# Fixed slots after the first two chunks in a routed mixture of experts behind a gated recurrence

## Chip, cores and metric

The kernel runs on one core of a Trainium2 chip. The metric is the device time of one execution in microseconds (us), lower is better; the median of several runs is compared.

## What is computed

A gated linear recurrence runs over 4 sequences of 5056 tokens with 256 features. Its 20224 output rows go through a mixture of 8 experts, where each token visits only the expert with the largest logit:

```python
log_a = c * sig_r * np.log(np.clip(a_base, 1e-06, 1.0 - 1e-06))[None, None, :]
a_t = np.exp(log_a)
x_gated = np.sqrt(np.maximum(1.0 - a_t * a_t, 1e-06)) * sig_i * x
for t in range(S):
    h = a_t[:, t] * h + x_gated[:, t]
    y[:, t] = h
...
logits = x @ w_gate                      # x: the 20224 rows of y
e_idx = np.argmax(logits, axis=1)
for e in range(E):
    mask = e_idx == e
    h = np.maximum(x[mask] @ w1[e], 0.0)      # 256 -> 1024
    ye = h @ w2[e]                            # 1024 -> 256
    out[mask] = gate_w[mask, None] * eom[mask, e, None] * ye
```

## The kernel before

**Chunks.** The 158 tiles of 128 tokens are cut into 20 chunks of 8 tiles (the last has 6). `chunk` loads the three inputs of half a chunk (`rt`, `it`, `xt`, 0.5 MB each), makes the gates on ScalarE (ACT) and VectorE (DVE), runs the recurrence as a scan on DVE, and then, tile by tile, transposes on TensorE (PE) against an identity that also carries the router's columns (`prow`). DVE and ACT split each row into a high and a low half of fp16 (`rows_all`), choose the expert, rank each token within its expert (`pk`, `posi`), and GpSimd (POOL) scatters the rows by an indirect DMA into `xs`, a table in device memory with one region of rows for each expert.

**Slots.** A slot is a piece of up to 256 or 128 rows of one expert. The counts are known only on the chip, so `plan` (DVE) works out for a group of slots which expert and which row each one takes; tokens that do not fill a slot wait for a later chunk. `slot` then fetches the rows with a transposing DMA (`xt16`), copies the expert's first weights (`ws`, two copies of 0.5 MB, from `w1r` in on-chip memory at an address read from the plan), multiplies 48 times for the first layer (`ph`), evacuates each fourth of it by a `relu` on ACT and a `low` on DVE (`h`), multiplies 24 times for each 128 rows for the second layer (`po`), scales on ACT (`ot`) and scatters the result on POOL. A slot of 256 rows is called wide here, one of 128 narrow. Before the change there are 63 wide and 39 narrow slots: 17 narrow ones after chunks 1 and 2, four wide ones after each of chunks 4 to 18, and 3 wide and 22 narrow ones at the end. The last 3 narrow slots stand under an `If` and run only if the first of them has rows.

**Weights.** Each of the 16 weight matrices (8 experts, two layers; 1 MB each) is a `unit`: it is loaded, measured (a Gram product on PE, `pg`, then a square on ACT and two small steps on DVE, `wsc`), and split into a high half (ACT, or DVE where `MODES` has a D) and a low half (DVE) that stay on the chip in `w1r` and `w2r`. Before, the first layers of all experts come first, then the second layers, and the first slot's weight copy waits for all first layers, its second layer for all units.

**Order.** Every step is a `work` item with a rank. `in_order` lays the items out on the engines by a planner whose costs are tables at the head of the file (`UNIT_RANK`, `CHUNK_RANK`, `SLOT_RANK` and so on). PE, ACT and DVE then run exactly in that order; SP's and POOL's queues follow it too. An engine therefore stands still when the next row of its list is not ready.

## Time and profile before

| | |
|---|---|
| median of 3 runs | 1089.17 us (1087.86 to 1091.37) |
| the profiled execution: its own time | 1083.89 us |
| its span, first to last instruction | 1082.2 us |
| PE / DVE / ACT / POOL busy | 990.1 / 732.1 / 633.8 / 345.7 us |
| mean granted clock of PE | 0.965 |

The profile is of one execution. Its own time lies 1.7 us above its span, and 0.5% below the median of the runs, so a sum made on the span has to be scaled to the median. Busy time is a union over an engine's instructions; where short instructions overlap in the pipeline, the sum of their durations is larger than the busy time.

### The profile page before, as it was taken

To read this page: it belongs to the slowest core of one execution; us is meant where nothing else is said; L and a number is where in the kernel's file an instruction comes from. 1 tells how busy PE (TensorE), PEld (TensorE's weight loads), DVE (VectorE), ACT (ScalarE), POOL (GpSimd) and SP (SyncE) were. 2 spreads that over 40 slices of the span, in tenths; PEclk is the share of its full clock that TensorE was granted. 3 is DMA by queue.
4 is the path that set the end of the run, shared out by engine and by line. 5 is a ranking of instruction groups with operands and counts; after the bars stand their busy time and mean duration, and the time that the engine had idled before them with its cause. 6 is when DMAs were issued, how large, how long until landed. Compare 5 with 4: busy or idle time off the path is not lost.

```text
span 1082.2 us, 29773 instructions
## 1 busy us (share of the span) xinstructions
PE 990.1 (91%) x9738; PEld 897.1 (83%) x9738; DVE 732.1 (68%) x2012; ACT 633.8 (59%) x1092; POOL 345.7 (32%) x346
## 2 busy tenths in 40 slices
PE   2445689999999999999999999999999999999997
PEld 2434578888998989989889899989999988899997
DVE  7999987869757777676777758677687544234332
ACT  9885866766756556566665657757565333223332
POOL 1033133233332423333243333334434444122111
PEclk9867699999999999999999999999999999999999
DMA  9992499999768697796968779787675555447993
GB/s 346 392 367 85 116 265 278 321 308 288 247 207 257 192 249 208 238 222 222 257 220 224 225 224 253 215 243 243 215 239 169 177 182 186 155 155 223 233 243 131
DMA packets 196862, 249.41 MB, mean 230 GB/s; under 512 B 120013, under 2 KB 128976, under 8 KB 196720
## 3 DMA queue, kind: packets, MB, share of 16 engines
q1 hardware_dynamic: 180928, 204.17, 64.4%
q0 software_dynamic: 15792, 43.31, 12.0%
q8 instruction: 94, 1.54, 0.6%
q14 instruction: 48, 0.39, 0.1%
...
## 4 chain that ended last, share of the span: by engine, by line
PE 41%; issue 20%; DMA 10%; POOL 8%; DVE 6%; SPq 3%; ACT 3%; POOLq 0%; ACTq 0%
PE po L933 19%; PE ph L889 19%; POOL xs L339 5%; DMA xs<-rows_all,posi 4%; DMA rt<-in_r_gate_dram 4%; POOL out_dram L948 3%; PE prow L598 3%; DVE h L907 2%; DMA ws<-w1r 1%; SPq L837 1%; DVE it L564 1%; DMA out_dram<-ot,mt 1%; ACT h L904 1%; ACT rt L511 1%; SPq L838 1%
## 5 line engine op out<-in xcount | busy, mean ns | idle before, releaser
L889 PE MATMUL ph<-xt,ws 128*128 128x256 f16 (+1 forms) x4752 | 524.8, 255 | 19.1 <-DVE h L907 12.2
L933 PE MATMUL po<-w2r,h 128*128 x3888 | 520.4, 273 | 2.4 <-ACT ot L945 0.9
L889 PEld LDWEIGHTS <-ws 128*128 128x128 f16 x4752 | 410.4, 99 | 61.8 <-issue 9.5
L933 PEld LDWEIGHTS <-h 128*128 128x128 f16 x3888 | 374.3, 98 | 44.8 <-issue 2.9
L907 DVE SCALAR_TENSOR_TENSOR h<-ph,h 128x512 f16<-128x512 f32 (+1 forms) x396 | 226.7, 589 | 210.5 <-ACT h L904 208.1
L948 POOL DMA_INDIRECT out_dram<-ot,mt x162 | 175.0, 1080 | 447.5 <-ACT ot L945 386.4
L904 ACT ACTIVATE h<-ph 128x512 f16<-128x512 f32 (+1 forms) x396 | 201.0, 518 | 155.9 <-PE po L933 109.4
L339 POOL DMA_INDIRECT xs<-rows_all,posi x158 | 158.5, 1003 | 270.9 <-ACT h L904 128.0
L598 PE MATMUL prow<-iw,it 128*128 128x144 f32 x632 | 112.2, 306 | 37.0 <-DVE it L564 20.2
L623 ACT ACTIVATE rows_all<-prow,sc 128x256 f16<-128x256 f32 x150 | 68.5, 473 | 116.2 <-DMA xs<-rows_all,posi 93.7
L945 ACT ACTIVATE ot<-po,osc 128x256 f32<-128x256 f32 x162 | 69.7, 471 | 106.5 <-PE po L933 94.4
L598 PEld LDWEIGHTS prow<-iw,it 128*128 128x128 f32 x632 | 92.9, 204 | 40.3 <-issue 32.8
L564 DVE TENSOR_TENSOR_SCAN it<-rt,last,it 128x512 f32<-128x512 f32 (+4 forms) x78 | 95.8, 1241 | 0.5
L627 DVE SCALAR_TENSOR_TENSOR rows_all<-prow,sc,rows_all 128x256 f16<-128x256 f32 x158 | 75.3, 477 | 0.0
L533 DVE SCALAR_TENSOR_TENSOR it<-it,xt 128x1024 f32<-128x1024 f32 (+1 forms) x40 | 48.3, 1207 | 24.0 <-ACT it L530 24.0
L612 DVE TENSOR_REDUCE am<-prow 128x1 f32<-128x256 f32 x158 | 59.5, 416 | 6.5 <-PE prow L598 6.5
L521 ACT ACTIVATE rt<-rt,lam 128x512 f32<-128x512 f32 (+1 forms) x80 | 60.8, 803 | 0.5
L626 DVE COPY lz<-prow 128x16 f32<-128x16 f32 x158 | 26.6, 169 | 50.3 <-ACT rows_all L623 50.1
L517 DVE SCALAR_TENSOR_TENSOR xt<-it,xt 128x1024 f32<-128x1024 f32 (+1 forms) x40 | 48.3, 1207 | 10.8 <-ACT it L514 10.6
L511 ACT ACTIVATE rt<-rt 128x1024 f32<-128x1024 f32 (+1 forms) x40 | 41.8, 1045 | 22.5 <-DMA rt<-in_r_gate_dram 21.5
L514 ACT ACTIVATE it<-it 128x1024 f32<-128x1024 f32 (+1 forms) x40 | 41.8, 1045 | 8.9 <-DMA it<-in_i_gate_dram 8.8
L530 ACT ACTIVATE it<-it,quarter 128x1024 f32<-128x1024 f32 (+1 forms) x40 | 45.2, 1138 | 0.3
...
## 6 DMA issues: line engine op xcount, KB each, us to landing
...
out_dram<-ot,mt POOLq DMA_INDIRECT x162, 3.6
xs<-rows_all,posi POOLq DMA_INDIRECT x158, 3.6
```

The costliest lines, as they stand in the source:

```text
L339: op = nc.gpsimd.indirect_dma_start(out=xs[:, :], out_offset=bass.IndirectOffsetOnAxis(ap=pos, axis=0), in_=rows.bitcast(F32), in_offset=None,
L521: nc.scalar.activation(r[:, h], r[:, h], AF.Exp, scale=lam[:, h:h + 1], bias=lam[:, h:h + 1])
L564: nc.vector.tensor_tensor_scan(H[:, h, lo:hi], A[:, h, lo:hi], H[:, h, lo:hi], first, op0=ALU.mult, op1=ALU.add)
L598: nc.tensor.matmul(pf[:, h * P:(h + 1) * P + 2 * E], lhsT=H[:, h, (j % 4) * P:(j % 4 + 1) * P], rhs=iw[:, h, :], start=h == 0, stop=h == N ...
L623: nc.scalar.activation(r4(j)[:, 0], pr(j), AF.Copy, scale=sc)
L627: nc.vector.scalar_tensor_tensor(r4(j)[:, 1], pr(j), st("sc", 1, I32)[:, j, :].bitcast(F32), r4(j)[:, 0], op0=ALU.mult, op1=ALU.subtract)
L889: nc.tensor.matmul(ph[:, i, 0:w], lhsT=ws[:, f // 2 % 2, a, c, i * P:(i + 1) * P], rhs=xt[:, b * ND + c, 0:w], start=k == 0, stop=k == 3 * ...
L904: newest["relu"] = nc.scalar.activation(part(0, f0), tiles["ph", s, f0][:, :, 0:w], AF.Relu).ins
L907: nc.vector.scalar_tensor_tensor(part(1, f0), tiles["ph", s, f0][:, :, 0:w], 0.0, part(0, f0), op0=ALU.max, op1=ALU.subtract)
L933: nc.tensor.matmul(po[0:pw, j], lhsT=hh[:, a, f % 4, j * P:j * P + pw], rhs=w2r[:, bass.ds(eo + (b * NF + f) * D, D)], start=f + j + a + b ...
L945: nc.scalar.activation(ot[0:pw], tiles["po", s][0:pw, j], AF.Copy, scale=tiles["osc", s][0:pw, j, :])
L948: op = nc.gpsimd.indirect_dma_start(out=out[:, :], out_offset=bass.IndirectOffsetOnAxis(ap=tiles["mt", s][0:pw, j, 1:2].bitcast(I32), axis=0),
```

## The change

After each of the first two chunks there are now 8 narrow slots of fixed place, one for each expert: slot k takes rows 0 to 127 (after chunk 1: rows 128 to 255) of expert k's region. They need no plan, no address registers and no `ws` copy, since place and expert are constants; they read `w1r` and `w2r` directly. So that a region that has too few tokens can be read, two `fill` DMAs write zero rows over the first 256 rows of each region, and the scatters of chunk 0 wait for them; `carry` is raised so that the next tokens go behind the fixed rows. The weights are split expert by expert, three experts ahead of the slots, and each fixed slot waits only for its own expert. Later slots come from a table, `CUTS`: 5 narrow after chunk 2, 7 after chunk 3, then 6, 5 and 4 slots after chunks 4, 5 and 6 to 10 (wide and narrow mixed), four wide ones after chunks 11 to 18, and 38 narrow ones at the end, of which 23 run always, 3 under an `If` and 12 under a second `If` inside it. Wide and narrow slots of a chunk are planned as two groups, and every plan now checks whether a slot is used. Together: 50 wide and 79 narrow slots in place of 63 and 39. The extra bytes are 2 x 1.08 MB of zero rows. Chunk 1 no longer borrows the buffers of `ws` and `hh` for its loads. All tables of ranks are new.

```diff
+STATIC = 2
+
+CUTS = {
+    2: ((128, 5),), 3: ((128, 7),), 4: ((256, 1), (128, 5)), 5: ((256, 2), (128, 3)), 6: ((256, 3), (128, 1)),
+    7: ((256, 3), (128, 1)), 8: ((256, 3), (128, 1)), 9: ((256, 3), (128, 1)), 10: ((256, 3), (128, 1)),
+}
+CUT = ((256, 4),)
+
+ENDS = (23, 3)
+AHEAD = 3
...
-SLOT_RANK = (-35.066, -22.048, -35.396, -20.11)
+SLOT_RANK = (-168.923, -171.768, -182.749, -176.243)
...
-        w = WIDTHS[c] if c < len(WIDTHS) and c < NC - 1 else SLOT
-        pending -= add_slots(c, max(0, -(-(pending - E * (w - 1)) // w)), w)
+        if c < STATIC:
+            add_slots(c, E, P)
+            pending -= min(pending, P)
+        elif c < NC - 1:
+            for w, k in CUTS.get(c, CUT):
+                add_slots(c, k, w)
+                pending = max(min(pending, E * (w - 1)), pending - k * w)
     n_full = len(width)
     add_slots(NC - 1, (pending + E * (P - 1)) // P, P)
     n_slots = len(width)
+    static = {s: (c, k) for c in range(STATIC) for k, s in enumerate(slots_in[c])}
...
+    def fill(r):
+
+        op = nc.sync.dma_start(
+            xs.rearrange("(e r) d -> r e d", e=E)[r * P:(r + 1) * P],
+            zrow.bitcast(F32).rearrange("p (o d) -> p o d", o=1).to_broadcast([P, E, ROW // 2]),
+        )
+        tc.declare_no_dep(op.ins, group="xs", reason="rows of xs are written before those of tokens")
+        tc.add_to_no_dep_group("xs", op.ins)
+        queue("SP", op)
+        scatters.append((-1, op.ins))
...
+        for k in [k for cc, k in scatters if cc < 0] if c == 0 else []:
+            tc.add_manual_dep(
+                ins, k.name, mybir.DependencyInfo(mybir.DependencyClass.Sync, mybir.DependencyReason.DATA),
+                reason="zero rows are written before those of tokens",
+            )
...
-    units = [(e, i) for i in range(2) for e in range(E)]
+    units = [(e, i) for e in range(E) for i in range(2)]
...
-            nc.vector.tensor_tensor(left, left, pk[:, nt * E:(nt + 1) * E], op=ALU.add)
+            if c >= STATIC:
+                nc.vector.tensor_tensor(left, left, pk[:, nt * E:(nt + 1) * E], op=ALU.add)
+                return
+
+            nc.vector.tensor_scalar(tab[:, 3, :], tab[:, 3, :], float(P), None, op0=ALU.add)
+            nc.vector.tensor_tensor(carry, carry, tab[:, 3, :], op=ALU.max)
+            if c == STATIC - 1:
+                nc.vector.tensor_tensor(left, carry, tab[:, 3, :], op=ALU.subtract)
...
-            if tail:
-                a = tile_of("pla", [GROUP, 1])[:, 0:n]
-                nc.vector.tensor_reduce(a, o, axis=AX.X, op=ALU.add)
-                nc.vector.tensor_tensor(v[:, :, 0:1], v[:, :, 0:1], step[w][:, 0:n, 0:1], op=ALU.add)
-                nc.vector.scalar_tensor_tensor(v[:, :, 0:1], v[:, :, 0:1], -float(dummy), a, op0=ALU.add, op1=ALU.mult)
-                nc.vector.tensor_scalar(v[:, :, 0:1], v[:, :, 0:1], float(dummy), None, op0=ALU.add)
-                nc.vector.tensor_copy(vi, v[:, :, 0:2])
-            else:
-                nc.vector.tensor_tensor(vi, v[:, :, 0:2], step[w][:, 0:n], op=ALU.add)
+
+            a = tile_of("pla", [GROUP, 1])[:, 0:n]
+            nc.vector.tensor_reduce(a, o, axis=AX.X, op=ALU.add)
+            nc.vector.tensor_tensor(v[:, :, 0:1], v[:, :, 0:1], step[w][:, 0:n, 0:1], op=ALU.add)
+            nc.vector.scalar_tensor_tensor(v[:, :, 0:1], v[:, :, 0:1], -float(dummy), a, op0=ALU.add, op1=ALU.mult)
+            nc.vector.tensor_scalar(v[:, :, 0:1], v[:, :, 0:1], float(dummy), None, op0=ALU.add)
+            nc.vector.tensor_copy(vi, v[:, :, 0:2])
...
+        w_ = work("DVE", 3.3, emit, [chain["plan"], old] + undone, -4.5 + s0 / 1000, uses=[use])
...
+        for w in sorted({width[s] for s in slots_in[c]}, reverse=True):
+            same = [s for s in slots_in[c] if width[s] == w]
+            if same[0] >= n_full:
+                cuts = [same[:ENDS[0]], same[ENDS[0]:sum(ENDS)], same[sum(ENDS):]]
+            else:
+                cuts = [same]
+            for part in cuts:
+                for k in range(0, len(part), GROUP):
+                    plan(part[k:k + GROUP])
...
-        ready, vuse = planned[s]
-        if s in rescaled:
-            rescaled["last"] = rescaled[s]()
-        scaled = rescaled["last"]
+        fixed = static.get(s)
+        ready, vuse = planned[s] if fixed is None else (counted[c], [])
+        expert = None if fixed is None else fixed[1]
+        scaled = undone[expert] if fixed else None
...
+                row = expert * REGION + fixed[0] * P
+                rows = xs[row:row + w]
...
-        rows = [v for cc in range(c + 1) for v in routed[cc]] if s == 0 or chunk_of[s - 1] != c else list(routed[c])
+        rows = list(routed[c])
...
+        every = [v for u in range(2 * E) for v in split[u]] if s == len(static) else []
...
+                    if fixed is None:
+                        ws = tiles["ws", s, f // 4]
+                    else:
+                        ws = w1r[:, expert * 2 * size + f // 4 * size:][:, 0:size].rearrange(
+                            "p (q h c f) -> p q h c f", q=2, h=2, c=ND
+                        )
...
-                deps = [wf[f0 // 4], fw] + ([pold] if i == 0 else [m])
+                deps = ([wf[f0 // 4]] if fixed is None else split[2 * expert]) + [fw] + ([pold] if i == 0 else [m])
...
-            m = work("PE", 0.327 * q, multiply2, [m, evac[f // 2], ready] + (every if f == 0 else []), rank + LAG + f / 1e4, uses=[pu, hus[f // 4][0], vuse])
+            m = work("PE", 0.327 * q, multiply2, [m, evac[f // 2], ready] + ((every if fixed is None else split[2 * expert + 1]) if f == 0 else []), rank + LAG + f / 1e4, uses=[pu, hus[f // 4][0], vuse])
...
+    fills = [work("SP", DMA_ISSUE, lambda r=r: fill(r), [tb], FILL, dma=3.0) for r in range(STATIC)]
...
-    for c in range(2):
+
+    def unscale(e):
+        nc.vector.reciprocal(undo[:, :, e:e + 1], wsc.bitcast(F32)[:, :, e:e + 1])
+        nc.vector.tensor_tensor(tab[:, 2, e:e + 1], undo[:, 0, e:e + 1], undo[:, 1, e:e + 1], op=ALU.mult)
+
+    def weights_of(e):
+        scaled = [unit(u, STAGED.get(u)) for u in (2 * e, 2 * e + 1)]
+        undone.append(work("DVE", 0.35, lambda: unscale(e), scaled, 3.5))
+
+    counted = {}
+    for c in range(NC):
         chunk(c)
-        plans(c)
-    scaled = [unit(u, STAGED.get(u)) for u in range(2 * E)]
-
-    def unscale():
-        nc.vector.reciprocal(undo, wsc.bitcast(F32))
-        nc.vector.tensor_tensor(tab[:, 2, :], undo[:, 0, :], undo[:, 1, :], op=ALU.mult)
-
-    undone[0] = work("DVE", 0.3, unscale, scaled, 3.5)
-    for c in range(NC):
-        if c > 1:
-            chunk(c)
+        counted[c] = chain["carry"]
+        if c >= STATIC:
             plans(c)
+        if c == 0:
+            for e in range(AHEAD):
+                weights_of(e)
         for s in slots_in[c]:
-            if s >= n_slots - SPARE and not late:
+            if c == 0 and s + AHEAD < E:
+                weights_of(s + AHEAD)
+            if s >= n_full + ENDS[0]:
                 late.append(s)
             slot(s)
...
+    k = n_full + sum(ENDS)
+    with where_used(n_full + ENDS[0]):
```

Where the tables move instructions shows in the order of the engines. The first place is SP's queue ahead of the first fetch of a slot's rows: in these rows `fw` and `w2r` are loads of weights, `ws` the copies of slot 0's weights, `xt_0_988` and `xt_0_579` the rows of slot 0, `mt` their scales, and `pvi` the plan. Before:

```order
L393 DMA fw_1_629<-in_moe_w_dram 128x4x256
L393 DMA fw_0_652<-in_moe_w_dram 128x4x256
L858 TENSOR_LOAD pvi_869
L863 ISA
L863 DMA ws_0_899<-w1r 128x2048
L863 ISA
L863 DMA ws_1_902<-w1r 128x2048
L505 DMA it_4_929<-in_i_gate_dram 128x2x512
L505 DMA xt_0_963<-in_x_dram 128x2x512
L830 TENSOR_LOAD pvi_869
L837 ISA
L837 DMA_TRANSPOSE xt_0_988<-xs 128x4x128
```

Now:

```order
L424 DMA w2r<-in_moe_w_dram 128x8x256
L424 DMA w1r<-in_moe_w_dram 128x2x1024
L424 DMA w2r<-in_moe_w_dram 128x8x256
L424 DMA w1r<-in_moe_w_dram 128x2x1024
L536 DMA xt_0_569<-in_x_dram 128x2x512
L424 DMA w2r<-in_moe_w_dram 128x8x256
L872 DMA_TRANSPOSE xt_0_579<-xs 128x4x128
L873 DMA mt_580<-xs 128x2
L872 DMA_TRANSPOSE xt_1_585<-xs 128x4x128
L873 DMA mt_586<-xs 128x2
L872 DMA_TRANSPOSE xt_2_596<-xs 128x4x128
L873 DMA mt_597<-xs 128x2
```

Slot 0's rows stood behind all loads of weights and behind the copy of its own weights, whose address is read from the plan; now they stand behind 14 of the 16 units, and no plan or copy stands ahead.

The second place is DVE around the first `low` of slot 0 (the row that makes `h_0` from `ph_0`). `lz` and `rows_all` belong to a chunk's rows, `mx` and `df` to its choice of experts. Before:

```order
L466 SCALAR_TENSOR_TENSOR w2r<-fw_0_529,wsc,w2r 128x1024
L466 SCALAR_TENSOR_TENSOR w2r<-fw_1_629,wsc,w2r 128x1024
L626 COPY lz_911<-prow_6_1017 128x16
L627 SCALAR_TENSOR_TENSOR rows_all<-prow_6_1017,sc_825,rows_all 128x256
L626 COPY lz_911<-prow_7_1075 128x16
L627 SCALAR_TENSOR_TENSOR rows_all<-prow_7_1075,sc_825,rows_all 128x256
L647 TENSOR_REDUCE mx_1127<-lz_911 128x8
L648 TENSOR_TENSOR df_1129<-lz_911,mx_1127 128x64
L432 TENSOR_SCALAR wsc<-pg_1082 128x1
L433 TENSOR_SCALAR wsc<-wsc 128x1
L907 SCALAR_TENSOR_TENSOR h_0_1131<-ph_0_1021,h_0_1131 128x2x128
L907 SCALAR_TENSOR_TENSOR h_0_1131<-ph_2_1043,h_0_1131 128x2x128
```

Now:

```order
L598 COPY last_4_631<-it_4_282 128x2
L643 TENSOR_REDUCE am_603<-prow_2_600 128x1
L643 TENSOR_REDUCE am_603<-prow_3_627 128x1
L645 TENSOR_SCALAR sc_604<-am_603 128x2
L548 SCALAR_TENSOR_TENSOR xt_0_569<-it_0_343,xt_0_569 128x1024
L947 SCALAR_TENSOR_TENSOR h_0_658<-ph_0_635,h_0_658 128x2x128
L657 COPY lz_615<-prow_2_600 128x16
L658 SCALAR_TENSOR_TENSOR rows_all<-prow_2_600,sc_604,rows_all 128x256
L657 COPY lz_615<-prow_3_627 128x16
L658 SCALAR_TENSOR_TENSOR rows_all<-prow_3_627,sc_604,rows_all 128x256
L1018 RECIPROCAL undo<-wsc 128x2
L1019 TENSOR_TENSOR tab<-undo 128x1
```

Before, the rows ahead of it are the last units' splits (`fw`) and the choice of experts of chunk 2; now chunk 1 is half done there, and the units of four experts are split (`undo` follows at once).

## Rows read from the trace of the kernel before

**Rows 1.** The page: span, busy time, granted clock in 40 slices of 27 us.

```profile
span 1082.2 us, 29773 instructions
...
PE 990.1 (91%) x9738; PEld 897.1 (83%) x9738; DVE 732.1 (68%) x2012; ACT 633.8 (59%) x1092; POOL 345.7 (32%) x346
...
PEclk9867699999999999999999999999999999999999
```

**Rows 2.** Windows: busy us (instructions) of each engine, granted clock, DMA share, GB/s.

```profile
0.00:80.00 80.00, 30.99 (x213) 28.00 (x213) 69.58 (x164) 68.27 (x91) 13.18 (x26) 0.81 1.02 369
80.00:120.00 40.00, 23.65 (x196) 21.69 (x197) 38.65 (x92) 25.29 (x42) 11.89 (x8) 0.69 0.32 102
120.00:160.00 40.00, 28.47 (x289) 25.84 (x288) 34.00 (x96) 28.96 (x48) 9.13 (x10) 0.79 0.70 201
160.00:200.00 40.00, 36.22 (x442) 33.02 (x441) 33.05 (x95) 28.07 (x52) 14.31 (x14) 0.96 1.05 298
200.00:1000.00 800.00, 794.20 (x7599) 717.28 (x7598) 532.78 (x1501) 456.67 (x794) 281.73 (x274) 1.00 0.76 224
```

**Rows 3.** Timeline of PE: the first slot's first layer (start, us, instruction, idle before).

```profile
117.02 4.00 PE L889 MATMUL ph<-xt,ws 128*128 128x128 f16 x36 [2.11 <-DMA xt<-xs]
...
130.78 1.46 PE L889 MATMUL ph<-xt,ws 128*128 128x128 f16 x12 [6.41 <-DVE h L907]
```

**Rows 4.** Timeline of PE at full clock: a row starts where the last is issued.

```profile
201.19 1.17 PE L889 MATMUL ph<-xt,ws 128*128 128x128 f16 x18
202.19 2.13 PE L933 MATMUL po<-w2r,h 128*128 x18
204.16 0.83 PE L889 MATMUL ph<-xt,ws 128*128 128x128 f16 x12
...
643.11 0.66 PE L598 MATMUL prow<-iw,it 128*128 128x144 f32 x4
643.61 2.13 PE L889 MATMUL ph<-xt,ws 128*128 128x256 f16 x18
645.57 0.82 PE L933 MATMUL po<-w2r,h 128*128 x6
```

**Rows 5.** Groups by form on PE: x count | busy us, mean ns | idle before.

```profile
L933 PE MATMUL po<-w2r,h 128*128 x3888 | 520.4, 273 | 2.4 <-ACT ot L945 0.9 <-ACT h L904 0.8 <-issue 0.7
L889 PE MATMUL ph<-xt,ws 128*128 128x256 f16 x3024 | 393.0, 273 | 3.1 <-DVE h L907 2.5 <-DMA ws<-w1r 0.3 <-DMA xt<-xs 0.2
L889 PE MATMUL ph<-xt,ws 128*128 128x128 f16 x1728 | 131.8, 224 | 16.0 <-DVE h L907 9.7 <-DMA ws<-w1r 3.9 <-DMA xt<-xs 2.1
```

**Rows 6.** Groups by form on DVE.

```profile
L907 DVE SCALAR_TENSOR_TENSOR h<-ph,h 128x512 f16<-128x512 f32 x252 | 169.4, 685 | 125.8 <-ACT h L904 124.6 <-issue 0.8
L564 DVE TENSOR_TENSOR_SCAN it<-rt,last,it 128x512 f32<-128x512 f32 x70 | 88.2, 1275 | 0.4
L627 DVE SCALAR_TENSOR_TENSOR rows_all<-prow,sc,rows_all 128x256 f16<-128x256 f32 x158 | 75.3, 477 | 0.0
L907 DVE SCALAR_TENSOR_TENSOR h<-ph,h 128x256 f16<-128x256 f32 x144 | 57.3, 421 | 84.7 <-ACT h L904 83.5 <-issue 0.7
L466 DVE SCALAR_TENSOR_TENSOR w1r<-w1r,wsc 128x1024 f16<-128x1024 f32 x12 | 14.8, 1280 | 1.1 <-ACT w1r L456 1.1
L466 DVE SCALAR_TENSOR_TENSOR w2r<-w2r,wsc 128x2048 f16<-128x2048 f32 x6 | 14.1, 2346 | 0.0
```

**Rows 7.** Timeline of DVE: first low of slot 0 and of slot 9.

```profile
130.31 0.74 DVE L907 SCALAR_TENSOR_TENSOR h<-ph,h 128x256 f16<-128x256 f32 x2
...
196.87 0.42 DVE L907 SCALAR_TENSOR_TENSOR h<-ph,h 128x256 f16<-128x256 f32 x1 [0.46 <-ACT h L904]
```

**Rows 8.** Timeline of POOL: first and last of chunk 0's eight scatters.

```profile
56.39 0.96 POOL L339 DMA_INDIRECT xs<-rows_all,posi  x1 [46.03 <-DVE am L612]
...
66.29 0.96 POOL L339 DMA_INDIRECT xs<-rows_all,posi  x1 [0.30 <-issue]
```

**Rows 9.** Timeline of PE: the last matmuls.

```profile
1072.63 4.09 PE L933 MATMUL po<-w2r,h 128*128 x36
```

More of the change, by code (lines that the diff above doesn't have):

```diff
@@ L478, in rglru_moe @@
     last_tile = {}
-    planned, rescaled, undone = {}, {}, {}
+    planned, undone = {}, []
     routed = {}
@@ L719, in chunk @@
         ps = work("DVE", 0.85, positions, [pk, chain["carry"]], quick, uses=[pu])
-        ct = work("DVE", 0.17, counts, [ps, chain["carry"]] + ([chain["plan"]] if chain["plan"] else []), quick, uses=[pu])
+        ct = work("DVE", 0.28 if c >= STATIC else 0.65, counts, [ps, chain["carry"]] + ([chain["plan"]] if chain["plan"] else []), quick, uses=[pu])
         chain["carry"] = ct
@@ L735, in chunk @@
             routed["ends"] = [
-                work("Pool", SPREAD[1], lambda e=e: scatter_rows(tiles["ends"][:, e:e + 1], zrow, NC), [w], quick, dma=0.38) for e in range(E)
+                work("Pool", SPREAD[2], lambda e=e: scatter_rows(tiles["ends"][:, e:e + 1], zrow, NC), [w], quick, dma=0.38) for e in range(E)
             ]
@@ L743, in plan @@
         s0, n, w = group[0], len(group), width[group[0]]
-        tail, early = s0 >= n_full, chunk_of[s0] < 2
+        tail = s0 >= n_full
         def tile_of(nm, shape, dt=F32, bufs=1):
@@ L753, in over_k @@
             return t.rearrange("p (o e) -> p o e", o=1).to_broadcast([P, n, t.shape[1]])
-        m = 2 if early else 3
+        m = 3
         def emit():
@@ L803, in plan @@
             planned[s] = (w_, use)
-        rescaled[s0] = lambda: work("DVE", 0.35, scales, [w_, undone[0]], -4.4 + s0 / 1000, uses=[use]) if early else w_
     def plans(c):
-        full = [s for s in slots_in[c] if s < n_full]
-        rest = slots_in[c][len(full):]
-        for group in (full, rest):
-            for k in range(0, len(group), GROUP):
-                plan(group[k:k + GROUP])
+        for w in sorted({width[s] for s in slots_in[c]}, reverse=True):
[7 more added lines that the diff above has]
+                    plan(part[k:k + GROUP])
     def slot(s):
@@ L916, in scales @@
             osc = tiles["osc", s] = small.tile([P, 2, 1], F32, name=f"osc_{s}", tag="osc", bufs=4)
-            nc.vector.tensor_scalar(osc[0:pw, 0:q, :], tiles["mt", s][0:pw, 0:q, 0:1], tiles["scale", s][0:pw], None, op0=ALU.mult)
-        sc = work("DVE", 0.2, scales, [scaled, fw, oold, evac[2]], rank, uses=[vuse, mu, ou])
+            by = tiles["scale", s][0:pw] if fixed is None else tab[:, 2, expert:expert + 1]
+            nc.vector.tensor_scalar(osc[0:pw, 0:q, :], tiles["mt", s][0:pw, 0:q, 0:1], by, None, op0=ALU.mult)
+        sc = work("DVE", 0.2, scales, [scaled, ready, fw, oold, evac[2]], rank, uses=[vuse, mu, ou])
         pu, pold = rings["ps_o"].new()
@@ L988, in rglru_moe @@
             w.emit()
-    newest.clear()
-    (row,) = (nc.values_load(
-        tiles["plan", late[0]][0:1, 0:1], min_val=0, max_val=E * REGION - P,
-        skip_runtime_bounds_check_because="rows are counted on the chip",
-    ),)
     rest = [w for w in works if w.late]
@@ L998, in rglru_moe, with where_used @@
     for w in rest:
-        w.after = [d for d in w.after if (isinstance(d, tuple) or id(d) in kept)]
-        w.after = [([x for x in d[0] if id(x) in kept], [x for x in d[1] if id(x) in kept]) if isinstance(d, tuple) else d for d in w.after]
-    with tc.If(row != dummy):
+        w.after = [d for d in w.after if isinstance(d, tuple) or id(d) in kept]
+        w.after = [tuple([x for x in k if id(x) in kept] for k in d) if isinstance(d, tuple) else d for d in w.after]
+    def where_used(k):
+        newest.clear()
+        row = nc.values_load(
+            tiles["plan", k][0:1, 0:1], min_val=0, max_val=E * REGION - P,
+            skip_runtime_bounds_check_because="rows are counted on the chip",
+        )
+        return tc.If(row != dummy)
+    k = n_full + sum(ENDS)
+    with where_used(n_full + ENDS[0]):
         with tc.manual_schedule(engines=engines):
-            for w in in_order(rest, {}):
+            for w in in_order([w for w in rest if w.late < k], {}):
                 w.emit()
+        if k < n_slots:
+            for w in rest:
+                w.after = [d for d in w.after if isinstance(d, tuple) or d.late >= k]
+                w.after = [tuple([x for x in q if x.late >= k] for q in d) if isinstance(d, tuple) else d for d in w.after]
+            with where_used(k):
+                with tc.manual_schedule(engines=engines):
+                    for w in in_order([w for w in rest if w.late >= k], {}):
+                        w.emit()
 _FEATURE_MAJOR = ("x", "r_gate", "i_gate")
```

112 lines of the change are left out of this document (54 added, 58 removed).

## The prediction

> **What bounds the kernel now.** I read the page first: PE is busy 91% of the span, and the row of its granted clock is low only in the first seven slices, about 190 us [rows 1]. The windows say the same in numbers [rows 2]: from 200 to 1000 us PE is busy 794.2 of 800 us, at full clock; in the first 200 us it is busy only 31.0 + 23.7 + 28.5 + 36.2 = 119.3 us, much of it at a mean granted clock of 0.69 to 0.81, a mixture of the two levels, 1.2 and 2.4 GHz. So two things can change the end: the amount of PE work, and how early PE has enough to do. In the first 200 us DVE is the busy engine (69.6 of 80, 38.7 of 40, 34.0 and 33.1 of 40). The timeline of PE then shows the first slot's multiplications only at 117.0 us, and they wait at 130.8 for a `low` of DVE [rows 3].
>
> **A unit for the sums.** At full clock a matmul costs, start to start [rows 4]: 128 columns (202.19 - 201.19) / 18 = 0.0556 us; `po` (204.16 - 202.19) / 18 = 0.1094 us, and 256 columns the same within 1% (645.57 - 643.61 over 18); the four records of one tile's `prow` 643.61 - 643.11 = 0.50 us. The ranking `pk` of a chunk is about 0.2 us (an estimate, nine short matmuls). A narrow slot is then 48 x 0.0556 + 24 x 0.1094 = 5.3 us, a wide one 96 x 0.1094 = 10.5 us.
>
> **More work for PE.** Before, 3888 matmuls of `po` and 3024 + 1728 of `ph` ran [rows 5]: 162 pieces of 128 rows in 99 slots, 63 wide and 36 narrow; the three under the `If` did not run. For the change I worked out the routing of the reference's data and put it through the table of slots: every planned slot finds a full piece, and 23 pieces are left for the end, exactly those that run always. So 50 wide and 64 narrow slots run, 164 pieces. That is 50 x 10.5 + 64 x 5.3 = 863.7 against 63 x 10.5 + 36 x 5.3 = 852.0: **11.7 us more**, certain, and at full clock, since PE has no idle time later in which to hide it. Two of the fixed slots' pieces are filler. The number of weight copies is nearly unchanged (98 planned slots against 99), so the stage after 200 us has no lighter DMA.
>
> **An earlier start, and who sets it.** DVE executes in the planner's order, so I added up the mean durations (busy over count, from the groups by form; the heaviest are in [rows 6]) of all DVE rows ahead of a given row. Ahead of slot 0's first `low` stand 129.4 us before the change, and the trace starts it at 130.3; ahead of slot 9's stand 195.0 us, and it starts at 196.9 [rows 7]. Up to there this sum reads as a clock: the overlap of short rows makes up for the tenth that DVE is idle. In the changed order the same sum is 68.1 us ahead of slot 0's `low` (21.9 of it splitting weights, 21.7 gates and scans, 12.6 rows of chunks 0 and 1), 130.9 ahead of slot 6's, 196.3 ahead of slot 16's and 292.4 ahead of slot 30's. So at about 196 us slot 16 takes the place that slot 9 had.
>
> From such a point the end follows from the PE work that its order still has ahead. Before, from slot 9's first `po`: 3687 x 0.1094 + 1248 x 0.0556 + 3024 x 0.1094 + 118 tiles x 0.5 + 3.3 = 865.9 us; 196.9 + 865.9 = 1062.8, and the last matmul ended at 1072.63 + 4.09 = 1076.7 [rows 9]. The 13.9 us between are the way from the `low` to the `po`, some 6 us of idle time and small gaps; I carry them over. The span ends 5.5 us after the last matmul; that too stays.
>
> Changed: slot 6, 899.7 us left: 130.9 + 899.7 + 13.9 + 5.5 = 1050.0. Slot 30, left 3192 x 0.1094 + 1614 x 0.0556 + 2352 x 0.1094 + 103 x 0.5 + 2.9 = 750.6: 292.4 + 750.6 + 19.4 = 1062.4. The largest of these counts: slots 20 to 30 of the changed order give 1060 to 1063, later ones less than 1058. So PE waits for DVE until about 290 us, longer than now, because the narrow slots, their plans (17 rows of DVE a group in place of 13, two groups for a mixed chunk) and chunks 2 to 5 all stand in that stretch. **Gain so far 1082.2 - 1062.4 = 19.8 us**, which already holds the 11.7 us.
>
> **What makes the start later than the sum.** DMA: ahead of slot 0's fetch in SP's queue stand 14 units (14.7 MB), 14 half-chunk loads (7.3 MB), the two fills (2.2 MB), and POOL moves 1.1 MB of chunk 0's rows: 25.3 MB, at the 369 GB/s of the first 80 us [rows 2] 68.6 us and some 2 us to begin, an estimate. So the rows of slot 0 land at about 71 to 73 us and the first `low` comes at about 75 to 77, not 68. The scatters do not set it: chunk 0's run from 56.4 to 67.2 us now [rows 8], and the positions that they wait for have 34 us of DVE sum ahead in place of 51, so even with the fills in front they end near 60. I also expect DVE to lie about 9 us behind its sum at the first positions, since with chunk 0 alone ready it waits for ACT's square roots and PE's transposes in turn. DVE can make up some of the 9 us where it is ready throughout (from 80 to 120 us it was busy 97% of the time [rows 2]); bounds are 0 and 9, I take 6, as no stretch of the trace shows it catching up by more than a few us. Span 1062.4 + 6 = 1068.4; own time 1.7 us more, 1070.1; scaled by 1089.17 / 1083.89 to the median, **1075 us**.
>
> Costs that I set at nothing: the three extra DVE rows of `counts` and the per-expert `undo` are in the sum; the second `If` stands inside the first, which is not entered; the extra plan groups at the end (six, not three) lie on DVE when it is far ahead. Without that cover each group would cost about 3 us once.
>
> **A rule that speaks against it.** The first slot ran at half rate: 36 matmuls of 128 columns took 4.00 us, 0.11 each, and the granted clock was 0.69 from 80 to 120 us [rows 2, 3]. The change moves 16 slots into such a stretch, where PE has waits between its bursts. The Trainium skill, "TensorE: Matmul & The Clock Gate", section "What's actually happening", has it that "the default state is throttled, and activity releases the throttle". By that rule, if the new stretch counts as too idle, its work takes up to twice the time; the trace agrees in so far as the clock rose to 0.96 once slots came one upon another. By the rows, PE has 51 us of full-rate work between slot 0 and slot 6 and DVE's sum gives it 63, so a little of this is hidden.
>
> **Rivals.** (a) The gain is larger: DVE catches up wholly after slot 6, and that slot binds: 1050.0 + 9 = 1059 span, 1066 median; with no lateness 1057. For it speaks that DVE's busy time is a tenth below its sum; against it, that the sum was the clock for 197 us. (b) DVE stays the bound. In chunks 6 to 10 its sum is about 40.8 us a chunk, and PE's work 3 x 10.5 + 5.3 + 8 x 0.5 + 0.2 = 41.0; before it was 37 against 46. No wait there is made up. If the order runs 5% behind its sum, slot 54 (sum 509.9, 528 us left) ends at 535.4 + 528 + 19.4 = 1083 span: 1090 median, no gain; at 8% it is 15 us more, slower. The turning point is 5%. For it: `low` waits for ACT's `relu` behind PE, which is already the largest wait of DVE [rows 6]. (c) The clock. If the 51 us run at 0.69, they take 74 and the span is 77 + 74 + 899.7 + 19.4 = 1070, within the forecast; at half clock 102 us, 1098, median **1105, slower**. It decides from a mean clock of 0.59 downward between 75 and 160 us. Against it: at 160 to 200 us the clock was 0.96 with PE 90% busy. (d) The early DMA is slow: at the 298 GB/s of 160 to 200 us [rows 2] the 25.3 MB take 85 us, the first `low` comes at 89, 12 us later, 1080 span, 1087 median: no change.
>
> **Chances.** Forecast 0.55 (median 1066 to 1086), (a) 0.18, (b) 0.14 (half of it slower), (c) 0.08, (d) 0.05. The range from 1058 to 1092 leaves out the tail of (a) below and most of (c) and the far part of (b) above. A measurement of this kernel tells about 0.3% from no change. Faster: the forecast but for its edge, and (a), 0.74; same: (d), part of (b) and that edge, 0.11; slower 0.15.
>
> **What would show it.** Right: first `ph` at 70 to 78 us; slot 16's first `low` near 200; PE's clock at 1.00 from about 140 us; PE busy some 10 us more in total; idle of PE for DVE's `low` spread until about 300 us and hardly any after. Wrong: a first `ph` after 85 us (fetch or fills), a granted clock near 0.5 up to 160 us, waits of PE for `low` that go on through chunk 10 (some 500 us), or the slots under the `If` running.

## The result and the profile after

The changed kernel takes **1078.41 us** (median of 4 runs, 1073.18 to 1081.11) beside 1088.51 us for the kernel before on the same chip: ratio **0.9904**, 95% interval 0.9875 to 0.9932. On a second chip it came to 1069.22 beside 1080.53 us, ratio 0.9886 (0.9870 to 0.9901). The forecast was 1075 us, with a range of 1058 to 1092. The profiled execution is the slowest of the four: own time 1081.11 us, span 1079.4 us. Spans of profiled executions therefore differ by only 2.8 us, where the medians differ by 10.1.

The page after, beside [rows 1]: PE is busy 11.4 us longer, close to the 11.7 us of added work, and the granted clock is low in slices 2 and 3 (27 to 81 us), and again a little in slice 5 (108 to 135 us) and slice 12 (about 300 us).

```profile
span 1079.4 us, 31430 instructions
...
PE 1001.5 (93%) x10506; PEld 910.0 (84%) x10506; DVE 772.4 (72%) x2324; ACT 642.5 (60%) x1153; POOL 361.7 (34%) x348
...
PEclk9659799999989999999999999999999999999999
```

The windows after, same stretches as [rows 2] (busy us of PE, its weight loads, DVE, ACT, POOL; granted clock; DMA share; GB/s):

```profile
0.00:80.00 80.00, 34.81 (x274) 31.27 (x275) 65.41 (x163) 55.75 (x81) 17.52 (x26) 0.74 1.04 349
80.00:120.00 40.00, 34.74 (x456) 32.35 (x454) 36.17 (x84) 32.84 (x62) 18.96 (x12) 0.98 0.59 134
120.00:160.00 40.00, 35.40 (x389) 32.02 (x388) 34.86 (x97) 30.80 (x56) 5.79 (x4) 0.85 0.49 135
160.00:200.00 40.00, 39.38 (x511) 36.79 (x509) 35.95 (x115) 27.17 (x50) 16.21 (x16) 1.00 0.71 177
200.00:1000.00 800.00, 784.79 (x7922) 709.38 (x7921) 568.13 (x1752) 468.85 (x840) 288.45 (x275) 0.99 0.81 237
```

In the first 200 us PE is now busy 144.3 us, against 119.3 before, and from 80 to 200 us at a higher clock (0.98, 0.85 and 1.00 in place of 0.69, 0.79 and 0.96); up to 80 us it is lower, 0.74 in place of 0.81. That is the gain. But from 200 to 1000 us it stands still 15.2 us, against 5.8 before. Cut finer, in the same view, first before, then after:

```profile
200.00:320.00 120.00, 117.17 (x1246) 106.66 (x1245) 90.10 (x268) 78.87 (x141) 39.15 (x39) 1.00 0.92 271
320.00:800.00 480.00, 477.14 (x4387) 429.71 (x4386) 348.79 (x934) 303.21 (x501) 175.47 (x168) 1.00 0.80 231
```

```profile
200.00:320.00 120.00, 110.72 (x1304) 100.44 (x1303) 91.78 (x312) 77.18 (x150) 44.53 (x40) 0.96 0.97 275
320.00:800.00 480.00, 474.28 (x4550) 427.03 (x4548) 388.55 (x1179) 321.16 (x543) 182.23 (x174) 1.00 0.86 247
```

9.3 us idle in the first in place of 2.8 before, 5.7 in the second in place of 2.9. A clock of 0.96 in place of 1.00 over the first 120 us means some 10 us at the lower level, which costs about 5 us more, an estimate. Both are given back, beside the added work. What PE waits for from 200 to 320 us (us in total, times, longest):

```profile
PE prow L629 <- DVE rows_all L658: 3.1, 1, 3.1
PE ph L929 <- DMA ws<-w1r: 2.1, 1, 2.1
PE po L982 <- ACT ot L994: 1.3, 1, 1.3
...
PE ph L929 <- DVE h L947: 0.8, 3, 0.3
```

The marks that the prediction named, in the timeline of DVE after (start, us; first lows of slots 0, 6, 16 and 30):

```profile
74.96 0.42 DVE L947 SCALAR_TENSOR_TENSOR h<-ph,h 128x256 f16<-128x256 f32 x1
...
137.51 0.76 DVE L947 SCALAR_TENSOR_TENSOR h<-ph,h 128x256 f16<-128x256 f32 x2
...
200.84 0.75 DVE L947 SCALAR_TENSOR_TENSOR h<-ph,h 128x256 f16<-128x256 f32 x2
...
304.33 0.75 DVE L947 SCALAR_TENSOR_TENSOR h<-ph,h 128x256 f16<-128x256 f32 x2
```

and in that of PE (start, us, idle before). The first slot comes at 73.00 us; the four `prow` behind a 3.11 us wait run at half rate, 1.12 us from start to start in place of 0.50 [rows 4]; the same again at 300 us. The granted clock is 0.54 from 125.84 to 136 us and 0.51 from 299.95 to 306 us:

```profile
73.00 1.44 PE L929 MATMUL ph<-xt,w1r 128*128 128x128 f16 x12 [1.55 <-DMA xt<-xs]
...
125.84 1.33 PE L629 MATMUL prow<-iw,it 128*128 128x144 f32 x4 [3.11 <-DVE rows_all L658]
126.96 2.15 PE L450 MATMUL pg<-fw 128*128 128x128 bf16 x16
...
299.95 1.33 PE L629 MATMUL prow<-iw,it 128*128 128x144 f32 x4 [3.09 <-DVE rows_all L658]
301.07 0.85 PE L929 MATMUL ph<-xt,ws 128*128 128x128 f16 x6
...
1068.65 3.77 PE L982 MATMUL po<-w2r,h 128*128 x33
```

### The profile page after: what moved, and what is told of

Its sections match the earlier page's. It is cut to its first block, busy times and chain, and to the rows that moved or that the text cites. A ratio compares the mean times of both kernels' runs of the same rounds, so it can differ in the third digit from the quotient of the medians.

```text
span 1079.4 us, 31430 instructions
## 1 busy us (share of the span) xinstructions
PE 1001.5 (93%) x10506; PEld 910.0 (84%) x10506; DVE 772.4 (72%) x2324; ACT 642.5 (60%) x1153; POOL 361.7 (34%) x348
## 4 chain that ended last, share of the span: by engine, by line
PE 59%; issue 10%; DMA 10%; DVE 9%; POOL 5%; ACT 4%; SPq 1%; POOLq 0%; ACTq 0%; DVEq 0%
PE ph L929 27%; PE po L982 27%; PE prow L629 5%; DMA xs<-rows_all,posi 3%; POOL xs L365 3%; DVE it L595 2%; POOL out_dram L997 2%; DVE h L947 2%; DMA rt<-in_r_gate_dram 2%; DMA w2r<-in_moe_w_dram 1%; DMA ws<-w1r 1%; DMA w1r<-in_moe_w_dram 1%; DMA xt<-xs 1%; DVE it L564 1%; ACT h L944 1%
## 5 line engine op out<-in xcount | busy, mean ns | idle before, releaser
L982 PE MATMUL po<-w2r,h 128*128 (+1 forms) x3936 | 533.3, 274 | 3.5 <-ACT ot L994 1.3
L929 PE MATMUL ph<-xt,ws 128*128 128x256 f16 (+1 forms) x4704 | 484.3, 247 | 5.1 <-DMA ws<-w1r 2.1
L929 PEld LDWEIGHTS <-ws 128*128 128x128 f16 x4704 | 384.4, 98 | 42.1 <-issue 4.6
L947 DVE SCALAR_TENSOR_TENSOR h<-ph,h 128x256 f16<-128x256 f32 (+1 forms) x456 | 240.1, 537 | 217.6 <-ACT h L944 187.8
L944 ACT ACTIVATE h<-ph 128x256 f16<-128x256 f32 (+1 forms) x456 | 211.8, 474 | 243.1 <-PE ph L929 150.4
L997 POOL DMA_INDIRECT out_dram<-ot,mt x164 | 180.9, 1103 | 434.6 <-ACT ot L994 313.9
L365 POOL DMA_INDIRECT xs<-rows_all,posi x158 | 168.5, 1066 | 264.3 <-ACT h L944 173.2
L994 ACT ACTIVATE ot<-po,osc 128x256 f32<-128x256 f32 x164 | 71.9, 471 | 54.9 <-PE po L982 49.4
L929 PE MATMUL ph<-xt,w1r 128*128 128x128 f16 x768 | 55.3, 225 | 4.6 <-DVE h L947 2.6
L929 PEld LDWEIGHTS <-w1r 128*128 128x128 f16 x768 | 50.6, 102 | 7.3 <-issue 6.0
```

Of the source, the lines that this page charges most:

```text
L365: op = nc.gpsimd.indirect_dma_start(out=xs[:, :], out_offset=bass.IndirectOffsetOnAxis(ap=pos, axis=0), in_=rows.bitcast(F32), in_offset=None,
L929: nc.tensor.matmul(ph[:, i, 0:w], lhsT=ws[:, f // 2 % 2, a, c, i * P:(i + 1) * P], rhs=xt[:, b * ND + c, 0:w], start=k == 0, stop=k == 3 * ...
L944: newest["relu"] = nc.scalar.activation(part(0, f0), tiles["ph", s, f0][:, :, 0:w], AF.Relu).ins
L947: nc.vector.scalar_tensor_tensor(part(1, f0), tiles["ph", s, f0][:, :, 0:w], 0.0, part(0, f0), op0=ALU.max, op1=ALU.subtract)
L982: nc.tensor.matmul(po[0:pw, j], lhsT=hh[:, a, f % 4, j * P:j * P + pw], rhs=second(b), start=f + j + a + b == 0, stop=f == NF - 1 and a == ...
L994: nc.scalar.activation(ot[0:pw], tiles["po", s][0:pw, j], AF.Copy, scale=tiles["osc", s][0:pw, j, :])
```

## Experiments

A **reading** used below, the prediction's own: the time of a slot's first `low` plus the full-rate PE work that stands behind it in the order. Where it is flat from slot to slot, PE loses nothing; where it rises, PE stood still or ran at half rate. Before it is 1049 us at slot 0, 1066 at slot 9, 1071 at the end. In the changed kernel (profile of the run `again`) it is about 1020 at slots 0 and 5, 1036 at slot 6, 1043 at slot 20, 1050 at slot 30, 1057 at slot 80 and 1061 at the end. So the head start by this reading is some 30 us up to slot 9, and some 20 of it are given back by the end; 8.8 us more idle after 200 us (14.6 against 5.8) and some 5 us for the lower clock, as estimated above, account for 14; the rest is not located. **Theory 1**: the gain is the earlier start, at the pace of DVE's order; DVE goes on to pace later slots and so gives part of it back. Each experiment has its rival. The kernel before ran again beside each group of runs, so times are compared by ratio. The yardstick is 0.9886; the first measurement of the same kernel gave 0.9904, so a difference of 0.2% says little.

**The unchanged kernel as yardstick (`again`).** No edit.

> The changed kernel unchanged, as a yardstick beside the others of this call. Its first profile was of the slowest of its four runs. Every theory expects the ratio of before, 0.990 within about 0.003, and a profile with a first low near 75 us, slot 6's near 137 us, and PE idle of 10 to 15 us after 200 us.

Measured: 0.9886 (0.9870 to 0.9901); first low at 74.8 us, slot 6 at 136.4, 14.6 us of PE idle from 200 to 1000 us. As expected.

**Without fixed slots.**

```diff
-STATIC = 2
+STATIC = 0
-    2: ((128, 5),), 3: ((128, 7),), 4: ((256, 1), (128, 5)), 5: ((256, 2), (128, 3)), 6: ((256, 3), (128, 1)),
+    0: (), 1: ((128, 9),), 2: ((128, 8),), 3: ((128, 7),), 4: ((256, 1), (128, 5)), 5: ((256, 2), (128, 3)), 6: ((256, 3), (128, 1)),
-ENDS = (23, 3)
-AHEAD = 3
+ENDS = (25, 3)
+AHEAD = 8
```

> No fixed slots: nine planned narrow slots after chunk 1 and eight after chunk 2 as before the change, which wait for all eight experts' weights; no zero rows are written; all other parts of the change stay (weights in expert order, table of cuts from chunk 3 on, checks in the plans, new ranks, two branches at the end). It runs 162 pieces of 128 rows, as before, so PE has about 10.5 us less to do than in the changed kernel. Theory 1 (the gain is the earlier start, paced by DVE's order): the sum of DVE's rows ahead of a slot's first low and of the PE work behind it is 1052 to 1059 us at slots 0 to 24 by the mean row durations of the trace before (1061 at slot 9 before, 1031 to 1043 at slots 6 to 30 in the changed kernel); with lows 5 to 10 us behind their sums, the first low stands at 132 to 138 us, the last matmul at 1070 to 1076 us, and the time at 1077 to 1087 us: most of what the earlier start gave is gone, and 10 us of PE work less hide it. Theory 2 (the gain comes from the other parts: expert order, cuts, ranks): the time stays at or under 1078 us, and under 1070 us when PE's lesser work counts in full.

Measured: 1101.49 us, ratio 1.0187 (1.0164 to 1.0210). Without the fixed slots the other parts bring nothing, so theory 2 falls. Beside the yardstick the kernel loses 3.0%, 32 us; that is more than the fixed slots are worth, since this kernel is also 1.9% slower than the one before, which has none either: its tables were made for other slots, and no run shows it with tables of its own. And theory 1 missed the size by 14 us or more. First low came at 136.5 us, as it said, the reading there is 1058 us, and it then rises to 1075 at slot 24, 1087 at slot 60 and 1093 at the end. The windows show the early part, to be read beside [rows 2]:

```profile
80.00:120.00 40.00, 13.63 (x80) 11.80 (x78) 36.11 (x79) 25.85 (x36) 4.26 (x5) 0.54 0.33 103
120.00:160.00 40.00, 30.43 (x324) 27.75 (x325) 34.55 (x123) 26.12 (x45) 9.73 (x10) 0.76 0.87 253
```

PE had little to do from 80 to 120 us and ran near half clock. After slot 24 another 18 us go. PE stands still 17.3 us from 200 to 1000 us, 8.5 of them for a `low`; why DVE is later there was not settled.

**The old number of later slots.**

```diff
-CUTS = {
-    2: ((128, 5),), 3: ((128, 7),), 4: ((256, 1), (128, 5)), 5: ((256, 2), (128, 3)), 6: ((256, 3), (128, 1)),
-    7: ((256, 3), (128, 1)), 8: ((256, 3), (128, 1)), 9: ((256, 3), (128, 1)), 10: ((256, 3), (128, 1)),
-}
+CUTS = {2: ((128, 5),), 3: ()}
```

> Fixed slots, expert order, fills, checks and ranks stay; only the table of later slots goes back to the number of before: 5 narrow slots after chunk 2, none after chunk 3, four wide ones after each chunk from 4 on, 23 narrow at the end. The PE work is that of the changed kernel (164 pieces), with 9 plan groups less. Theory 1 (the head start lasts only if the chunks that follow hand PE more slots): after the 21 slots of chunks 0 to 2 PE waits for the first slot of chunk 4; the sum of DVE's rows ahead of slot 21's first low and the PE work behind it is 1055 us against 1042 us, so the time is 5 to 15 us above the changed kernel's, ratio 0.994 to 1.003 to before, with PE idle in the stretch from 200 to 300 us well above the 7.5 us of the changed kernel. Theory 2 (the added cuts cost more in plans and narrow slots than they bring): the time falls by 3 us or more, ratio at or under 0.986.

Measured: 1.0039 (1.0018 to 1.0059), at the upper end of theory 1 and just past it; theory 2 falls. The start is the same (slot 6 at 136.2 us), and then PE runs dry. First the window 200 to 320 us of this kernel, then that of `again`:

```profile
200.00:320.00 120.00, 102.99 (x973) 90.69 (x970) 95.90 (x289) 80.30 (x135) 44.55 (x42) 0.93 0.83 248
```

```profile
200.00:320.00 120.00, 112.11 (x1353) 102.68 (x1351) 95.78 (x325) 79.27 (x156) 42.72 (x40) 0.97 0.99 286
```

17.0 us idle in place of 7.9, at a lower clock. The head start pays only because the chunks behind it hand out more slots: without that it is all given back (1.5%, 17 us). The ranks are those of the changed kernel here too.

**The weights in the old order.** The units go by layer, then by expert; each fixed slot waits for its two units.

```diff
-    units = [(e, i) for e in range(E) for i in range(2)]
+    units = [(e, i) for i in range(2) for e in range(E)]
...
```

> The fixed slots stay, but the weights are loaded and split in the order of before: the first layers of all experts, then the second layers. Theory 1 (DVE's order paces the early slots): the sum of DVE's rows ahead of each slot's first low is the one of the changed kernel within 3 us from slot 6 on (128 against 131 us at slot 6, 230 against 231 at slot 21), so the time is that of the changed kernel within 4 us, whatever slots 0 to 5 do. Theory 2 (the order by expert is what the early start needs): slot 0's second layer waits for the ninth unit in place of the second, PE stands still from about 75 to 110 us, later slots are late by 10 us or more, and the time is at 1088 us or above.

Measured: 0.9961 (0.9947 to 0.9976), 0.75% or 8 us above the yardstick, between the theories. Slot 2's first low comes at 107.2 us instead of 86.6, as theory 2 said; at slot 6 the kernel is level again (132.6 against 136.4 us), as theory 1 said, but at slot 22 it is 8 us behind (244.2 against 236.0 us) and the reading there 1051 against 1041 us. From 130 to 245 us PE stands still 10.0 us against 4.1, 5.5 of them for a `low` (0.9 in `again`). So the order by expert is worth something, and the loss lies between slots 6 and 22; why DVE is later there is not shown. The two profiled spans differ by only 2.0 us because that of `again` is its slowest of five (1072.9 us, the others 1063.9 to 1068.1), that of `by_kind` about its median.

**No check in the plans; wide slots only from chunk 4 on.** The first gives non-tail plans back their single `tensor_tensor`; the second is

```diff
-CUTS = {
-    2: ((128, 5),), 3: ((128, 7),), 4: ((256, 1), (128, 5)), 5: ((256, 2), (128, 3)), 6: ((256, 3), (128, 1)),
-    7: ((256, 3), (128, 1)), 8: ((256, 3), (128, 1)), 9: ((256, 3), (128, 1)), 10: ((256, 3), (128, 1)),
-}
+CUTS = {2: ((128, 5),), 3: ((128, 7),), 4: ((256, 3),), 5: ((256, 3),), 6: ((256, 3),)}
...
-ENDS = (23, 3)
+ENDS = (22, 3)
```

> The plans of slots that stand before the tail leave out the check whether a slot is used (every one of them is used with this input), as before the change: four DVE rows of about 0.2 us less in each of 24 plan groups, 16 of them ahead of slot 60. DVE's order is otherwise the same. Theory 1 in its strong form (DVE also paces the slots from 20 to 60): the sum at slot 30 falls by 7 us and at slot 54 by 18 us, so the time falls by 4 to 8 us, to 1070 to 1074 us, and the plateau of first low plus PE work left (1055 to 1058 us at slots 30 to 34) falls with it. Theory 2 (from slot 6 on PE alone sets the end): within 2 us of the changed kernel.

> As the changed kernel up to chunk 3; after chunks 4, 5 and 6 three wide slots each and after every later chunk four wide ones, so that no chunk has two plan groups; 22 narrow slots at the end. The same 164 pieces, the same pieces or one less handed out by each chunk from 4 to 10, seven plan groups less. Theory 1 (PE's end is set by the rows up to slot 6 and by waits of ACT and PE near 200 to 300 us, DVE's total does not count): within 3 us of the changed kernel. Theory 2 (the mixed groups and narrow slots of chunks 4 to 10 are what gives part of the gain back): 4 to 8 us faster than the changed kernel, ratio at or under 0.985.

Measured: 0.9898 (0.9878 to 0.9919) and 0.9885 (0.9864 to 0.9905): no difference. Without the check DVE has 68 rows less ahead of slot 56, some 11 us by their mean durations (ahead of slot 54 some 10, not the 18 that was expected), but the first low there moves only from 544.1 to 540.8 us, and the end not at all. After slot 30 DVE's rows do not set PE's pace, so theory 1 as stated above (DVE paces later slots; theory 2 in the text of `wide_cuts`) is wrong in that part.

**Transfers or DVE at the start.** Zero rows three times over; and ten idle reductions on DVE behind chunk 0's positions.

```diff
-    fills = [work("SP", DMA_ISSUE, lambda r=r: fill(r), [tb], FILL, dma=3.0) for r in range(STATIC)]
+    fills = [work("SP", DMA_ISSUE, lambda r=r: [fill(r + k) for k in (0, 162, 164)], [tb], FILL, dma=3.0) for r in range(STATIC)]
```

```diff
             nc.vector.tensor_tensor(carry, carry, pk[:, nt * E:(nt + 1) * E], op=ALU.add)
+            for k in range(10 if 0 <= c < 1 else 0):
+                nc.vector.tensor_reduce(pad, ones32.rearrange("p (o e) -> p o e", o=1).to_broadcast([P, 4, P]), axis=AX.XY, op=ALU.max)
```

> Each of the two DMAs of zero rows is followed by two more of the same size to rows that nobody reads: 4.3 MB more early on, and chunk 0's scatters wait for all of them. The order on PE, DVE and ACT is the same. The DMA engines moved 29.6 MB in the first 85 us, at their full share up to 66 us, so 4.3 MB take about 11 us at 380 GB/s. Theory 1 (the start is paced by DVE's order, and the transfers come early enough): first low and slot 6 move by under 3 us, the time by under 2 us. Theory 2 (the start is paced by the transfers as much as by DVE): first ph, first low and slot 6's low come 8 to 11 us later, and the time rises by 6 to 11 us, of which each fill of the change costs about 2.8 us.

> Ten idle reductions of 512 elements on DVE (about 0.7 us each by the 0.418 us of the reduction of 256, so 6 to 7 us in all) behind chunk 0's positions, ahead of slot 0's lows; nothing else differs in the order. Theory 1 (DVE's order paces the start): slot 0's and slot 6's first lows move by 5 to 7 us and the time rises by as much. Theory 2 (DVE waits for transfers there and has slack): slot 0's first low moves by under 2 us, slot 6's too, and the time by under 2 us.

Measured: 1.0008 (0.9985 to 1.0032) and 0.9919 (0.9906 to 0.9932). With the fills, POOL's first scatter and slot 0's first low, which stand at 43.21 and 74.82 us in `again`:

```profile
55.91 1.57 POOL L365 DMA_INDIRECT xs<-rows_all,posi  x1 [46.46 <-DVE tab L743]
```

```profile
87.56 0.42 DVE L947 SCALAR_TENSOR_TENSOR h<-ph,h 128x256 f16<-128x256 f32 x1
```

Both 12.7 us later for 4.3 MB, 2.9 us a MB; slot 6 is 13.4 us later, and the whole of it reaches the end (1.2%, 13 us). Of the pads

```profile
41.95 7.17 DVE L741 TENSOR_REDUCE pad<-ones 128x1 f32<-128x512 f32 x10
```

6.1 us arrive at slot 0's first low (80.92 us), 3.8 at slot 6 and about 3.6 at the end. So a delay of the zero rows, which chunk 0's scatters wait for, arrives in full, and rows of DVE's arrive in part: theory 1's "DVE" was about half of it. The 3.6 us are the weak figure here: beside 0.9904 they would be 1.6. At 2.9 us a MB the change's own fills (2.16 MB) cost about 6 us, an estimate.

**Fewer zero rows**, only where this input leaves rows empty:

```diff
-            xs.rearrange("(e r) d -> r e d", e=E)[r * P:(r + 1) * P],
+            xs.rearrange("(e r) d -> r e d", e=E)[(64, 176)[r]:(r + 1) * P],
...
```

> The zero rows are written only over rows 64 to 127 and 176 to 255 of each region, which covers all rows that this input leaves empty: 1.22 MB in place of 2.16 MB; nothing else differs. The trebled fills cost 12 to 13 us for 4.3 MB, 2.9 us for each MB. Theory 1 (transfers pace the start): 0.94 MB less bring first low and slot 6 forward by 2 to 3 us and the time down by as much, ratio about 0.986. Theory 2 (the trebled fills only overran a slack that the changed kernel's fills stay inside, and DVE's order sets the start now): within 1 us of the changed kernel, ratio 0.988 to 0.990.

Measured: 0.9877 (0.9853 to 0.9902). The time cannot tell the theories apart; in the profile slots 0 to 6 come 1.9 to 2.1 us earlier, as theory 1 said, but slot 20 is later again than in `again` (229.1 against 225.6 us).

**Scatters not spread.** This took aim at the 3.09 us wait at 300 us above, where ACT waits for chunk 5's spread scatters to land.

```diff
-        if c >= PACED[0] and "relu" in newest:
+        if c >= 8 and "relu" in newest:
```

> The scatters of chunks 2 to 7 no longer wait for a relu each, so they leave one after the other; all orders are the same. In the changed kernel chunk 5's eight scatters are spread from 275 to 304 us, ACT's copies of chunk 6's rows wait for their landing (3.8 and 3.6 us at 283 to 293 us), the relus behind them stand still, and PE idles 3.4 us at 300 us. Theory 1 (this spreading is part of what is given back after slot 6): the step of 5 to 9 us in first low plus PE work left between slots 29 and 31 goes, and the time falls by 3 to 6 us, ratio 0.983 to 0.986. Theory 2 (the wait covers a lateness of DVE or PE, or the bunched scatters delay weight copies by as much): within 2 us of the changed kernel.

Measured: 1.0072 (1.0049 to 1.0095), 1.9% or 20 us slower than the yardstick; both theories missed. The wait for landing shrinks from 21.8 to 6.5 us, but a new one appears. ACT's waits from 190 to 450 us (us in total, times, longest), here and in `again`, where the first line does not exist:

```profile
ACT h L944 <- remote: 26.3, 7, 5.5
ACT h L944 <- PE ph L929: 26.2, 30, 2.4
...
ACT rows_all L654 <- DMA xs<-rows_all,posi: 6.5, 2, 6.4
```

```profile
ACT h L944 <- PE ph L929: 27.4, 35, 2.1
ACT rows_all L654 <- DMA xs<-rows_all,posi: 21.8, 9, 6.2
```

The timeline of all engines without the spreading shows where it lies:

```profile
241.03 0.96 POOL L365 DMA_INDIRECT xs<-rows_all,posi  x1 [0.30 <-DVE h L947]
...
242.30 0.96 POOL L365 DMA_INDIRECT xs<-rows_all,posi  x1 [0.30 <-issue]
...
243.57 1.08 POOL L365 DMA_INDIRECT xs<-rows_all,posi  x1 [0.30 <-issue]
...
244.95 0.96 POOL L365 DMA_INDIRECT xs<-rows_all,posi  x1 [0.31 <-issue]
...
245.53 0.27 PE L982 MATMUL po<-w2r,h 128*128 x1 [1.06 <-issue]
...
247.06 0.94 ACT L944 ACTIVATE h<-ph 128x256 f16<-128x256 f32 x3 [4.83 <-remote]
```

Four scatters run back to back, and while they do ACT stands 4.83 us and PE in gaps of up to 1.06 us for which the trace shows no releaser (20 such gaps of PE, 0.2 to 2.4 us long, 14.4 us in all, from 190 to 450 us; none in `again`).

**Edits together.** Wide slots, no check and fewer zero rows; and, besides, the last spare plans moved under the first branch:

```diff
             for i, part in enumerate(cuts):
+                if i == 2:
+                    late.append(n_full + ENDS[0])
                 ...
+                if i == 2:
+                    late.pop()
```

> Three edits together: wide slots only from chunk 4 on (22 narrow ones at the end), no check in the plans before the tail, and the smaller fills. The first two moved nothing alone. Theory 1: only the fills' 2 to 3 us show, ratio 0.985 to 0.987. Theory 2 (each edit alone ran into the next limit, so DVE's rows count once two of them are gone): 6 us or more under the changed kernel, ratio at or under 0.983.

> The kernel with the three edits (wide slots only from chunk 4, no check before the tail, smaller fills), and besides the plans of the last 12 spare slots moved into the first of the two branches, which this input does not take. In the kernels of the change so far a plan of three slots is DVE's last work, up to the end of PE's last matmul, and 6.6 to 7.0 us pass from that matmul's end to the end of the span, against 5.5 us before the change. Theory 1 (the late plan holds up the branch): the tail falls to 5.5 us and the time by 1 to 1.5 us, ratio to before 0.982 to 0.987. Theory 2 (the second branch itself costs the difference): the tail stays at 6.6 us and the ratio at 0.985.

Measured: 0.9854 (0.9831 to 0.9877) and 0.9852 (0.9820 to 0.9885). The first came out as its theory 1 said; its gain over the yardstick, 0.3%, is at the edge of what can be told. The moved plans did not help, as theory 2 of the second said: the last matmul starts its record as below, ends 3.77 us later at 1063.96 us, and the span is 1070.4 us, a tail of 6.4 us, though DVE now ends at 1061.2. That the second branch itself costs the difference to 5.5 us was not tested.

```profile
1060.19 3.77 PE L986 MATMUL po<-w2r,h 128*128 x33
```

## Why the prediction held, step by step

- **Added PE work, 11.7 us**: right. Busy time rose by 1001.5 - 990.1 = 11.4 us, and 3936 `po` ran, 24 for each of 164 pieces, so neither branch was entered.
- **Earlier start**: right in place and size. First `ph` at 73.0 us (70 to 78 said), first low 75.0 (75 to 77), slot 16's at 200.84 (near 200), chunk 0's scatters end at 58.4 us (near 60). `no_fixed` shows that the fixed slots bring it.
- **Who sets it**: half right. I let DVE's sum be the clock and the DMA a delay of slot 0 that DVE catches up. `fills_thrice` shows that a delay by the zero rows is not caught up at all, `pad_start` that DVE's own rows count for about half.
- **The sum**: short in three terms of the span, all the same way, and near the measured median in part by luck. In the profiled execution slot 30's first low is at 304.3, not 292.4 + 6: the lateness is 11.9 us. From there 750.6 us of work end at 1072.4 (1068.65 + 3.77): 17.5 us are carried, not 13.9. The tail is 7.0 us, not 5.5. Together 5.9 + 3.6 + 1.5 = 11.0 us, and 1068.4 + 11.0 is the span, 1079.4. In `again` the three are 7.2, 16.2 and 6.5 us, together 4.5 us above the forecast. The forecast of the median missed by 3.4 us only, because scaling to the median had added 5.2 us, which stand for no mechanism, and because the profiled run lies 2.7 us above its median.
- **The carried 13.9 us** came in part from a misread row: the low at 196.87 us [rows 7] is slot 8's last; slot 9's first is at 199.74, so the kernel before carried 11.1 us, and DVE was 4.7 us behind its sum of 195.0 there, not 1.9. The sum was less of a clock than it was taken for, and read rightly the forecast would have been 2.8 us lower, further from the result.
- **"PE waits for DVE until about 290 us, hardly any after"**: right in place, wrong in what PE waits for. The idle time concentrates there (9.3 us from 200 to 320 us), but 5.7 us more lie up to 800. And the sign named was a wait for DVE's `low`: from 200 to 320 us that ends 0.8 us of it, the `prow` behind the wait of ACT at 300 us 3.1, weight copies 2.1 and a result on ACT 1.3. `no_check` and `wide_cuts` show that these are not DVE's total, so rival (b), DVE as the bound up to chunk 10, is out.
- **Lateness made up?** I gave DVE the choice between 0 and 9 us and took 6. Up to slot 20 it was 4 to 8 us late; at slots 29 to 31 the wait at 300 us added the rest.
- **Rival (c), the clock**: it did not decide. The granted clock was 0.98 from 80 to 120 us and 0.85 from 120 to 160 us, far from the 0.59 that would have cost the gain. What the prediction left out lies later: about 5 us from 200 to 320 us (an estimate, above), where it had full rate. By the Trainium skill, "TensorE: Matmul & The Clock Gate", section "What's actually happening", "the default state is throttled, and activity releases the throttle"; the trace agrees in the two stretches of half rate behind waits of 3.1 us, and these are part of the terms above.
- **Rival (d), slow early DMA**: not so here (349 GB/s in the first 80 us), but that bytes ahead of slot 0 move the end is shown by `fills_thrice`.
- **Chances**: the forecast and (a) add up to 0.73, so "faster" could not be 0.74.

Open: what exactly the 5.7 us of small waits from 320 to 800 us hang on, why `by_kind` falls behind after slot 6, and why `no_fixed` does after slot 24.
